# K of eleven head pairs loaded in chunk rows and transposed by DMA, Q in long rows re-laid by GpSimd, in a chunk-select attention with a gated MLP

## The chip, the cores and the metric

The kernel runs on one core of one Trainium2 chip. Its metric is the device time of one launch in microseconds (us); lower is better. Five engines work side by side, each through its own list of instructions in order: TensorE (PE) multiplies matrices and transposes into PSUM, VectorE (DVE) and ScalarE (ACT) read PSUM and SBUF, GpSimd (POOL) reads and writes SBUF, SyncE (SP) issues the DMA transfers, which 16 DMA engines carry out.

## The reference, cut to what matters

Attention over 32 pairs of batch and head (B = 4, H = 8, S = 768, D = 64), in which every query keeps the six best of the 24 chunks of 32 keys, and then an MLP with a hard-swish gate:

```python
k_chunks = k.reshape(B, H, nc, chunk, D)             # chunk = 32, nc = 24
k_min = np.min(k_chunks, axis=3)
k_max = np.max(k_chunks, axis=3)
ub = np.sum(np.maximum(q[:, :, :, None, :] * k_min[:, :, None, :, :],
                       q[:, :, :, None, :] * k_max[:, :, None, :, :]), axis=-1)
ub = np.where(causal, ub, -1000000000.0)
top_chunks = np.argsort(ub, axis=-1)[..., -top_k:]    # top_k = 6
scores = scale * np.matmul(q, k.transpose(0, 1, 3, 2))
scores = np.where(sel & (pos[:, None] >= pos[None, :]), scores, -1000000000.0)
attn = softmax(scores)
x = (attn @ v), heads side by side                    # 3072 x 512
h = x @ w_in                                          # 512 -> 2048
out = (h * np.clip(h + 3.0, 0.0, 6.0) / 6.0) @ w_out  # 2048 -> 512
```

## The kernel before, in words

Two heads of one batch make a pair; there are 16 pairs, four to a batch. Heads stand side by side on the 128 partitions (64 dimensions each). The MLP works on groups of 384 rows, eight of them, two to a batch; a group can begin once the four pairs of its batch have that half of their rows.

All work stands in one list, `ORDER`, written out by hand. A token such as `S.3.5.b` names an operation, its pair or group, its part and the PSUM slot it uses. Every engine takes its own tokens in the order of the list; waits come from what a token reads and overwrites. Two things therefore set the order around the change: the list, and the buffers. PSUM has three large slots, a, b and c (`PSB`, two banks each), and two small ones, x and y (`PSS`, one bank each).

For a pair `i` the tokens are:

- `lk`, `lq`, `lv` (L199 to L206): SP loads K, Q and V, two DMAs each, one for a head, in pieces of 64 numbers (256 bytes), so that a partition holds six positions 128 apart. Each of the three has three buffers (`KS`, `QS`, `VS`).
- `K`, `Q` (L263, L267): six transposes of 128 x 128 on TensorE into a large slot. `kb`, `qb` (L272, L275): ScalarE copies them as bf16 into `KB`, `QB` (three buffers each). `mx`, `mn` (L278): VectorE takes the maximum and the minimum of K over each chunk of 32 columns of that slot, into `KM`. `rp`, `rn` (L283, L286): the positive and the negative part of Q from column 192 on (the first six chunks need no choice).
- `U` (L296): the bounds, 24 small fp32 matmuls. `ub`, `T`, `t8`, `sel`, `L`, `mt`: causal bias, transposition, the eight largest, the comparison with the sixth, transposition back, and the mask rows `MT`.
- `S.i.u` (L368): the scores in six units, and `ex` (L382): their exponentials on ScalarE into `PT`.
- The mask goes in by one of two ways. Pairs without `sm` tokens (0 to 5) add it in PSUM by further matmuls with `EM` (L376), and GpSimd cuts the diagonal of the exponentials (`af`, L389). Pairs with `sm` (6 to 15, `PRODUCT`) write the mask rows to a scratch in HBM, four DMAs (L341), read them back widened over the partitions, six DMAs (`ml`, L346), into `MX` (parts of it lie in the weight buffers `WS`); GpSimd cuts the diagonal of that mask (`am`, L353), and VectorE multiplies the exponentials with it (`mu`, L360).
- `vc` (L251): GpSimd casts V. `A`, `B` (L405): values; `na`, `nb` (L422, L425): the division by the sums, into `XB`.

For a group `g`: `X` and `xe`, or three DMA transposes (`xt`, L431), turn `XB` into `XT`; `H` (L449, eight matmuls of 384 columns, 8 tokens to a group), `hu` (ScalarE, L457), `gt` (VectorE, L460), `O` (L466, four matmuls of 512 columns; four tokens make one 128-row output tile), `ot` (ScalarE, L474), `st` (L478, the store). Weights come through `wl` (SP) and `wc` (GpSimd).

Of the kernel before, what the change touches and what calls it, by code (L numbers as in the profile page):

```python
# [15 lines left out]
P = 128  # L16
# [18 lines left out]
PRD PRP lk.0 Z.b.14 PRA PRL K.0.a kb.0 mx.0 mn.0 lq.0 Q.0.b rp.0 qb.0 rn.0 lk.1 K.1.c kb.1 mx.1 lq.1 Q.1.a rp.1  # L35
qb.1 mn.1 lq.2 U.0.b ub.0 T.0.x Q.2.c rp.2 qb.2 rn.1 U.1.b lk.2 K.2.a kb.2 t8.0 sel.0 ub.1 L.0.y mt.0 S.0.5.b
rn.2 mx.2 mn.2 T.1.x ex.0.5 S.0.1.c ex.0.1 lq.3 lk.3 lv.0 vc.0 af.0.1 S.0.0.b ex.0.0 S.0.3.c ex.0.3 S.0.2.a
ex.0.2 U.2.b S.0.4.c ex.0.4 lv.1 t8.1 sel.1 L.1.y ub.2 T.2.x mt.1 S.1.1.b ex.1.1 S.1.4.a Q.3.c ex.1.4 S.1.0.b
t8.2 sel.2 L.2.y rp.3 qb.3 K.3.a kb.3 rn.3 af.0.0 af.0.3 af.0.2 af.0.5 B.0.0.x B.0.1.x mt.2 lq.4 lv.2 lk.5 lk.4
wl.0 lq.5 wl.1 ex.1.0 S.1.2.c ex.1.2 S.2.2.b ex.2.2 A.0.y mx.3 mn.3 S.1.5.c ex.1.5 S.1.3.a U.3.b ex.1.3 na.0  # L40
nb.0 ub.3 S.2.3.c ex.2.3 S.2.1.a S.2.0.b ex.2.1 ex.2.0 T.3.y t8.3 vc.1 af.1.0 vc.2 sel.3 af.1.1 af.1.2 af.1.3
af.1.5 af.2.2 K.4.c kb.4 mx.4 S.2.5.a ex.2.5 af.2.5 B.1.0.x af.2.1 af.2.3 Q.4.b rp.4 qb.4 L.3.y B.1.1.x mt.3
S.3.3.a ex.3.3 mn.4 rn.4 A.1.y S.2.4.c ex.2.4 nb.1 S.3.1.b ex.3.1 na.1 U.4.a S.3.0.c ex.3.0 S.3.5.b ub.4 T.4.x
t8.4 sel.4 wc.0 af.2.0 ex.3.5 af.3.5 wc.1 Q.5.a rp.5 S.3.2.c ex.3.2 X.0.0.y xe.0.0 K.5.b L.4.x mt.4 qb.5 lq.6
lk.6 lv.3 kb.5 B.2.0.y S.4.3.c rn.5 af.3.1 af.3.2 af.3.0 wl.2 B.2.1.y S.4.1.a vc.3 X.1.0.x ex.4.3 ex.4.1 S.4.2.c
ex.4.2 lv.4 wl.3 S.4.4.a ex.4.4 mx.5 mn.5 U.5.b af.3.3 wc.2 S.3.4.c xe.1.0 nb.2 ub.5 A.3.x na.3 ex.3.4 S.4.0.b
ex.4.0 vc.4 af.4.1 T.5.y t8.5 sel.5 Q.6.a rp.6 S.4.5.c ex.4.5 K.6.b L.5.x mt.5 B.3.0.y qb.6 rn.6 kb.6 mx.6 mn.6
S.5.2.c ex.5.2 A.2.x na.2 S.5.1.a ex.5.1 B.3.1.y nb.3 S.6.3.c ex.6.3 S.5.3.a ex.5.3 af.4.0 wc.3 U.6.b ub.6
S.6.0.c ex.6.0 A.4.x na.4 S.5.5.a S.6.1.b ex.5.5 ex.6.1 af.4.5 af.5.3 af.5.2 af.4.3 X.1.1.y xe.1.1 T.6.x wl.4
af.5.1 af.6.1 wc.4 S.6.4.c ex.6.4 lv.5 S.5.0.a ex.5.0 af.5.0 af.5.5 vc.5 lk.8 lk.7 lq.7 S.5.4.b ex.5.4 t8.6  # L50
X.0.1.y xe.0.1 sel.6 af.4.2 H.1.7.c H.0.7.a hu.1.7 gt.1.7 H.1.2.b wl.6 lq.8 hu.0.7 gt.0.7 L.6.y mt.6 sm.6 wl.5
hu.1.2 gt.1.2 K.7.c kb.7 mx.7 mn.7 B.5.0.x H.0.2.a hu.0.2 gt.0.2 H.0.1.b hu.0.1 A.5.y na.5 Q.7.c rp.7 gt.0.1
qb.7 rn.7 H.1.0.a wc.6 B.4.0.y B.4.1.y hu.1.0 S.6.2.b gt.1.0 ml.6.5 ml.6.2 ml.6.4 lv.7 wc.5 wl.7 lv.6 vc.7
ex.6.2 S.7.0.c ex.7.0 B.5.1.x nb.5 U.7.a ub.7 ml.6.0 ml.6.3 ml.6.1 K.8.b kb.8 nb.4 S.7.1.c ex.7.1 mx.8 mn.8
H.1.4.a hu.1.4 gt.1.4 H.1.3.c hu.1.3 gt.1.3 T.7.x t8.7 H.1.6.b H.0.6.a hu.1.6 gt.1.6 hu.0.6 H.0.4.c H.0.0.b
sel.7 gt.0.6 L.7.y hu.0.4 gt.0.4 Q.8.a mt.7 am.6.5 wc.7 af.6.0 vc.6 am.6.4 hu.0.0 gt.0.0 H.0.5.c H.0.3.b rp.8
qb.8 rn.8 hu.0.5 gt.0.5 U.8.a hu.0.3 sm.7 lk.9 S.8.4.c ex.8.4 am.6.2 am.6.3 ub.8 gt.0.3 O.0.2.0.x T.8.y t8.8
sel.8 S.6.5.a ex.6.5 lq.9 S.8.3.c S.7.5.b ml.7.1 ml.7.2 am.7.2 ml.7.3 ml.7.5 af.7.0 am.7.3 ml.7.0 mu.6.5 mu.6.1
# [12 lines left out]
S.10.0.a ex.10.0 S.10.5.c ex.10.5 O.1.1.0.y ex.11.1 T.11.x O.1.1.1.y am.9.4 am.9.3 t8.11 sel.11 mu.9.1 S.9.4.a
ex.9.4 am.9.2 mu.9.4 mu.9.5 S.11.0.c ex.11.0 S.10.1.b ex.10.1 O.1.1.2.y O.1.1.3.y ot.1.1 L.11.x S.11.5.a af.10.1
vc.9 am.9.5 ex.11.5 S.11.3.c K.12.b kb.12 ex.11.3 af.11.1 O.1.0.0.y ml.10.2 lv.10 ml.10.5 ml.10.4 af.10.0
am.10.4 am.10.5 mu.9.3 Q.12.a O.1.0.1.y mu.9.0 mu.9.2 mt.11 rp.12 mx.12 mn.12 H.2.7.c A.9.x hu.2.7 gt.2.7 vc.10
am.10.2 qb.12 rn.12 O.1.0.2.y O.1.0.3.y ot.1.0 S.11.2.b S.10.3.c ex.10.3 na.9 ex.11.2 U.12.a ub.12 B.9.0.y
B.9.1.y ml.10.3 am.10.3 mu.10.5 nb.9 S.10.4.c ex.10.4 S.12.3.a S.12.2.b ex.12.2 ex.12.3 O.2.2.0.x O.2.2.1.x
st.1.2 lq.14 ml.10.0 lk.13 lq.13 sm.11 lk.14 lv.11 ml.11.1 st.1.1 ml.11.3 ml.11.2 ml.11.0 mu.10.2 mu.10.0
mu.10.4 S.11.4.c S.12.5.b T.12.y t8.12 vc.11 ex.11.4 K.13.a kb.13 ex.12.5 O.2.2.2.x O.2.2.3.x ot.2.2 sel.12
mu.10.1 S.12.0.c S.12.1.b ex.12.0 ex.12.1 A.10.y xt.3 mu.10.3 B.10.0.x B.10.1.x am.11.3 af.12.0 am.11.2 af.12.1
af.11.0 mx.13 Q.14.c rp.14 mn.13 ml.11.5 nb.10 na.10 Q.13.b K.14.a kb.14 ml.11.4 st.2.2 O.2.0.0.x O.2.0.1.x  # L80
L.12.y mx.14 mn.14 qb.14 rp.13 qb.13 rn.14 mt.12 O.2.0.2.x O.2.0.3.x rn.13 ot.2.0 mu.11.0 mu.11.5 mu.11.1 st.2.0
st.1.0 lq.15 S.13.0.a S.13.2.c O.2.1.0.y ex.13.0 O.2.1.1.y ex.13.2 S.13.3.b ex.13.3 S.12.4.a am.11.4 am.11.5
S.13.4.c ex.13.4 A.11.x O.2.1.2.y na.11 xt.4 ex.12.4 U.13.b ub.13 U.14.c O.2.1.3.y mu.11.2 ub.14 T.13.x t8.13
# [31 lines left out]
def kernel(  # L115
# [83 lines left out]
    def load_k(i):  # L199
        load(KS[i % 3], k, i)  # L200

    def load_q(i):
        load(QS[i % 3], q, i)

# [321 lines left out]
```

## Time and profile before

| What | Value |
|---|---|
| median of 3 runs | 287.31 us (286.42 to 288.61) |
| the profiled execution, its own time | 287.24 us |
| its span on the core | 285.2 us |
| granted TensorE clock | 0.998 |
| first matmul of the MLP (H.1.7) | 56.5 us |
| last DMA out of the mask scratch | about 215 us |

The profile is one execution; its times are microseconds from the span's start. A row of a group gives the line, the engine, the operation, output and input by the program's names, the count, then the busy time and the mean in nanoseconds, and behind the second bar the time that the engine idled just before and what ended it. "SPq" is the DMA queue of SyncE at its issuing work. A row of a stage gives the stretch, its length, and then how long PE, its weight loads (PEld), DVE, ACT and POOL were busy in it, the granted clock, the mean share of the 16 DMA engines, and GB/s. The chain of work that ended last is followed backwards from the last instruction, at each step to what released it.

### The profile page before, as it was taken

Reading aid. Unit: us, or ns where it says so; the run is one execution under the profiler, and the core shown is the slowest. Engines: PE = TensorE matmul, PEld = TensorE weight load, DVE = VectorE, ACT = ScalarE, POOL = GpSimd, SP = SyncE. Lnnn points to the kernel's source line nnn. Section 1 sums busy time; section 2 is a strip of 40 time slices with the busy share of each in tenths; the row PEclk is TensorE's granted clock in tenths of the full one; section 3 lists DMA queues with packets and bytes.
Section 4 is the critical chain, followed back from the end, with each engine's and each line's share of the span. In section 5 each row is a group of like instructions: output and inputs, shape, how many; then the busy total and the mean of one; then the engine's idle time right before and its main releaser. Section 6 shows DMA issues by size and latency. Waiting matters only on the chain.

```text
span 285.2 us, 7112 instructions
## 1 busy us (share of the span) xinstructions
PE 273.7 (96%) x2782; PEld 165.5 (58%) x2782; DVE 205.1 (72%) x535; ACT 179.3 (63%) x234; POOL 72.5 (25%) x133
## 2 busy tenths in 40 slices
PE   8699999999999999999999889999999999999994
PEld 4467777667656576665574456555546645554541
DVE  4997787978989888989696788689748933251430
ACT  2599999977678874768787465352586324422521
POOL 6026575742450502314303100062422000000000
PEclk9999999999999999999999999999999999999999
DMA  8999999998999999979989958999594023110102
GB/s 169 218 214 191 344 219 305 288 261 239 261 247 253 224 254 213 231 206 274 245 184 233 259 105 173 271 255 237 148 280 142 12 47 93 74 39 37 61 15 110
DMA packets 107169, 54.40 MB, mean 191 GB/s; under 512 B 87168, under 2 KB 96128, under 8 KB 107136
## 3 DMA queue, kind: packets, MB, share of 16 engines
q1 hardware_dynamic: 107136, 53.95, 79.3%
q8 instruction: 22, 0.36, 0.6%
q14 instruction: 11, 0.09, 0.2%
HBM read 42.34 MB, written 9.24 MB: 181 GB/s over the span
## 4 chain that ended last, share of the span: by engine, by line
PE 61%; SPq 12%; DMA 9%; ACT 8%; DVE 4%; issue 4%; POOL 1%; ACTq 0%; POOLq 0%
PE PSx L466 13%; PE PSy L466 9%; PE PBa L449 7%; PE PBb L449 6%; PE PBc L449 6%; ACT PT L382 5%; SPq L346 4%; DMA VS<-in_v_dram 4%; SPq L341 3%; PE PSy L405 3%; SPq L197 3%; PE PBc L368 2%; DMA WS<-SCR 2%; PE PBb L368 2%; PE PBa L256 2%
## 5 line engine op out<-in xcount | busy, mean ns | idle before, releaser
L449 PEld LDWEIGHTS <-WIN 128*128 128x128 bf16 x512 | 49.1, 98 | 34.3 <-issue 2.5
L466 PEld LDWEIGHTS <-GT 128*128 128x128 bf16 x384 | 35.5, 98 | 39.6 <-issue 4.2
L466 PE MATMUL PSx<-WOUT,GT 128*128 128x512 bf16 x208 | 50.3, 379 | 0.0
L466 PE MATMUL PSy<-WOUT,GT 128*128 128x512 bf16 x176 | 43.5, 379 | 0.2 <-ACT OT L474 0.2
L382 ACT ACTIVATE PT<-PBc 128x1024 bf16<-128x1024 f32 (+2 forms) x38 | 37.0, 973 | 7.7 <-PE PBc L368 7.0
L449 PE MATMUL PBa<-XT,WIN 128*128 128x384 bf16 x176 | 32.2, 326 | 0.8 <-DMA XT<-XB 0.8
L460 DVE SCALAR_TENSOR_TENSOR GT<-U,PBc 128x768 bf16<-128x768 bf16 x21 | 20.0, 951 | 16.1 <-ACT U L457 16.1
L360 DVE TENSOR_TENSOR PT<-PT,WS 128x768 bf16<-128x768 bf16 (+2 forms) x70 | 30.3, 473 | 1.7 <-POOL WS L353 1.6
L449 PE MATMUL PBb<-XT,WIN 128*128 128x384 bf16 x168 | 30.7, 326 | 0.6 <-ACT PT L382 0.6
L449 PE MATMUL PBc<-XT,WIN 128*128 128x384 bf16 x168 | 30.7, 326 | 0.2 <-DVE UBX L301 0.2
L457 ACT ACTIVATE U<-PBa 128x768 bf16<-128x768 f32 x22 | 17.8, 810 | 20.8 <-PE PBa L449 19.5
L460 DVE SCALAR_TENSOR_TENSOR GT<-U,PBb 128x768 bf16<-128x768 bf16 x21 | 19.9, 949 | 14.0 <-ACT U L457 13.8
L405 PEld LDWEIGHTS <-PT 128*128 128x128 bf16 x672 | 24.6, 97 | 7.1 <-issue 1.4
L382 ACT ACTIVATE PT<-PBa 128x1024 bf16<-128x1024 f32 (+2 forms) x29 | 26.9, 927 | 2.1 <-PE PBa L368 2.1
L389 POOL TENSOR_SCALAR_AFFINE_SELECT PT<-PT 128x256 bf16<-128x256 bf16 x56 | 23.4, 439 | 15.6 <-ACT PT L382 15.6
L382 ACT ACTIVATE PT<-PBb 128x1024 bf16<-128x1024 f32 (+2 forms) x29 | 24.7, 852 | 2.7 <-PE PSy L405 1.8
L460 DVE SCALAR_TENSOR_TENSOR GT<-U,PBa 128x768 bf16<-128x768 bf16 x22 | 20.9, 949 | 7.6 <-ACT U L457 7.4
L457 ACT ACTIVATE U<-PBb 128x768 bf16<-128x768 f32 x21 | 17.0, 810 | 13.7 <-PE PBb L449 13.0
L457 ACT ACTIVATE U<-PBc 128x768 bf16<-128x768 f32 x21 | 17.0, 811 | 13.1 <-PE PBc L449 10.5
L353 POOL TENSOR_SCALAR_AFFINE_SELECT WS<-WS 128x256 bf16<-128x256 bf16 x30 | 13.3, 456 | 47.0 <-DMA WS<-SCR 46.8
L251 POOL CAST VB<-VS 128x768 bf16<-128x768 f32 x16 | 13.8, 862 | 38.1 <-DMA VS<-in_v_dram 35.9
L368 PEld LDWEIGHTS <-KB 64*128 64x128 bf16 x320 | 14.3, 94 | 13.0 <-issue 8.0
(103 smaller groups left out, 395.4 us busy)
## 6 DMA issues: line engine op xcount, KB each, us to landing
KS<-in_k_dram SPq DMA_DIRECT2D x32, 192.0 KB, 4.5
QS<-in_q_dram SPq DMA_DIRECT2D x32, 192.0 KB, 4.4
VS<-in_v_dram SPq DMA_DIRECT2D x32, 192.0 KB, 5.1
out_dram<-OT SPq DMA_DIRECT2D x24, 256.0 KB, 3.3
WS<-in_moe_w_in_dram SPq DMA_DIRECT2D x4, 1024.0 KB, 7.9
WS<-in_moe_w_out_dram SPq DMA_DIRECT2D x4, 1024.0 KB, 7.0
SCR<-MT SPq DMA_DIRECT2D x40, 72.0 KB, 3.2
MX<-SCR SPq DMA_DIRECT2D x10, 288.0 KB, 5.5
```

What stands on the lines that cost most here:

```text
L251: nc.gpsimd.tensor_copy(VB[i % 4][:, :, :, 0:D], VS[i % 3][:])
L346: nc.sync.dma_start(MX[i % 2][j][:, FIRST[j]:], src.unsqueeze(1).to_broadcast([16, 8, 2 * NQ - FIRST[j]]))
L353: nc.gpsimd.affine_select(out=T, in_=T, pattern=[[0, 2], [1, P]], compare_op=A.is_ge, fill=0.0, base=0, channel_multiplier=-1)
L360: nc.vector.tensor_tensor(out=T, in0=T, in1=mask_view(i, j, lo, q0 + n), op=A.mult)
L368: nc.tensor.matmul(PSB[c][:, e, at:at + n], lhsT=K[rows, j * P:(j + 1) * P], rhs=Q[rows, q0:q0 + n], start=True, stop=q0 + n <= Q0 or i in ...
L382: nc.scalar.activation(PT[i % 3][u][:, :, 0:n], PSB[slot["S", i, u]][:, :, 0:n], ACT.Exp, scale=float(scale))
L389: nc.gpsimd.affine_select(out=T[:, :, lo:lo + P], in_=T[:, :, lo:lo + P], pattern=[[0, 2], [1, P]], compare_op=A.is_ge, fill=0.0, base=0, ...
L405: nc.tensor.matmul(O[:, e, t, :], lhsT=PT[i % 3][u][:, e, lo:lo + P], rhs=VB[i % 4][:, j, e, :], start=(j == 0), stop=(j == qb))
L449: nc.tensor.matmul(PSB[c][:, ff, 0:GRP], lhsT=WIN[:, kt, (2 * f + ff) * P:(2 * f + ff + 1) * P], rhs=XT[g % 3][:, kt, :], start=(kt == 0), ...
L457: nc.scalar.activation(slot["R", g, f][:], PSB[slot["H", g, f]][:, :, 0:GRP], ACT.Relu, bias=3.0)
L460: nc.vector.scalar_tensor_tensor(out=GT[g % 2][:, 2 * f:2 * f + 2, :], in0=slot["R", g, f][:], scalar=6.0, in1=PSB[slot["H", g, f]][:, :, ...
L466: nc.tensor.matmul(PSS[c][:], lhsT=GT[g % 2][:, f, t * P:(t + 1) * P], rhs=WOUT[:, f, :], start=(f == 0), stop=(f == FT - 1))
```

## The change: what it does

Five things change together.

1. K of pairs 5 to 15 is loaded by one DMA into `KA`, 96 partitions with eight consecutive positions of both heads each (pieces of 2,048 bytes). VectorE takes maximum and minimum over the eight positions there (in SBUF, `MM`), TensorE transposes the two results into a small slot (two transposes of 96 columns), and VectorE reduces those by four to a chunk (`km`). GpSimd casts the rows to bf16 (`kc`, into the one buffer `KNB`), SP stores them to a scratch in HBM (`ks`), and a DMA transpose of 768 rows brings them into `KB` (`kt`). ScalarE's copy `kb` and the six transposes are not made for these pairs.
2. Q of all pairs is loaded by one DMA in pieces of 1,536 bytes (six consecutive positions of a head to a partition, two buffers `QA`). GpSimd re-lays it with the heads side by side (`qi`) into one buffer `QS`. After the transposition the columns stand in another order, so ScalarE (`qb`, `rp`) and VectorE (`rn`) read PSUM with a step of 128 columns.
3. V is loaded by one DMA in place of two, and has two buffers in place of three.
4. The mask goes by multiplication from pair 8 on; pairs 6 and 7 add it by matmul.
5. `ORDER` is written anew.

```diff
 ORDER = """
-PRD PRP lk.0 Z.b.14 PRA PRL K.0.a kb.0 mx.0 mn.0 lq.0 Q.0.b rp.0 qb.0 rn.0 lk.1 K.1.c kb.1 mx.1 lq.1 Q.1.a rp.1
...
-X.0.1.y xe.0.1 sel.6 af.4.2 H.1.7.c H.0.7.a hu.1.7 gt.1.7 H.1.2.b wl.6 lq.8 hu.0.7 gt.0.7 L.6.y mt.6 sm.6 wl.5
...
+PRD Z.b.14 PRP PRA PRL lk.0 K.0.a kb.0 mx.0 mn.0 lq.0 qi.0 Q.0.b rp.0 qb.0 rn.0 lk.1 K.1.c kb.1 lq.1 qi.1 Q.1.a
...
+B.0.0.x vc.1 lv.3 B.0.1.x lv.2 kc.5 qb.3 rn.3 af.1.1 S.1.5.a nb.0 ex.1.5 mt.2 S.1.0.b ex.1.0 mn.5 mx.5 S.1.4.a
+ex.1.4 S.1.2.b ex.1.2 A.0.x lq.5 lk.7 lk.6 ks.5 na.0 kb.4 U.3.a S.2.3.b ub.3 ex.2.3 mx.4 af.1.0 af.1.5 af.1.2
...
+mn.8 xe.1.1 xe.0.1 K.8.x km.8 X.0.0.y xe.0.0 ex.6.4 ex.6.3 Q.7.c af.5.1 af.5.3 qi.8 lq.10 kc.9 wc.2 af.4.0 wl.4
+mx.9 lv.6 mn.9 B.5.0.x A.5.y B.5.1.x lk.10 kt.7 ks.9 Q.8.b rp.7 qb.7 rn.7 na.5 rp.8 qb.8 rn.8 H.1.7.a hu.1.7
...
-    KS = ring(3, [P, NBLK, 2, D], FP32, "KS")
-    QS = ring(3, [P, NBLK, 2, D], FP32, "QS")
-    VS = ring(3, [P, NBLK, 2, D], FP32, "VS")
+    KP = S // 8
+    KSM = const.tile([P, 3 * S], FP32, name="KSM")
+    KS = [KSM[:, S * n:S * (n + 1)].rearrange("p (j e d) -> p j e d", e=2, d=D) for n in range(3)]
+    KA = [KSM[0:KP, 1024 * n:1024 * (n + 1)].rearrange("p (e k d) -> p e k d", e=2, d=D) for n in range(2)]
+    KNB = const.tile([KP, 8, 2, D], BF16, name="KNB")
+    MM = const.tile([KP, 2, 2, D], FP32, name="MM")
+    ROWQ = {int(t.split(".")[1]) for t in ORDER if t.startswith("qi.")}
+    QA = ring(2, [P, 2, NBLK, D], FP32, "QA") if ROWQ else []
+    QS = ring(1 if ROWQ else 3, [P, NBLK, 2, D], FP32, "QS")
+    VS = ring(2, [P, 2, NBLK, D], FP32, "VS")
...
+    ROWK = sorted({int(t.split(".")[1]) for t in ORDER if t.startswith("kt.")})
+    SK = {i: dram.tile([S, P], BF16, name=f"SK{i}") for i in ROWK}
...
     def load_k(i):
-        load(KS[i % 3], k, i)
+        if i in ROWK:
+            b, hp = divmod(i, NPAIR)
+            nc.sync.dma_start(KA[i % 2].rearrange("p e k d -> p e (k d)"),
+                              k[b, 2 * hp:2 * hp + 2].rearrange("e (p k) d -> p e (k d)", k=8))
+        else:
+            load(KS[i % 3], k, i)
+
+    def k_cast(i):
+        nc.gpsimd.tensor_copy(KNB[:], KA[i % 2].rearrange("p e k d -> p k e d"))
+
+    def k_store(i):
+        nc.sync.dma_start(SK[i][:].rearrange("(p k) c -> p (k c)", k=8), KNB[:].rearrange("p k e d -> p (k e d)"))
+
+    def k_turn(i):
+        nc.sync.dma_start_transpose(KB[i % 3][:], SK[i][:])
 
     def load_q(i):
-        load(QS[i % 3], q, i)
+        if i in ROWQ:
+            b, hp = divmod(i, NPAIR)
+            nc.sync.dma_start(QA[i % 2][:].rearrange("p e j d -> p e (j d)"),
+                              q[b, 2 * hp:2 * hp + 2].rearrange("e (p j) d -> p e (j d)", j=NBLK))
+        else:
+            load(QS[i % 3], q, i)
+
+    def q_interleave(i):
+        nc.gpsimd.tensor_copy(QS[0][:], QA[i % 2][:].rearrange("p e j d -> p j e d"))
 
     def load_v(i):
-        load(VS[i % 3], v, i)
+        b, hp = divmod(i, NPAIR)
+        nc.sync.dma_start(VS[i % 2][:].rearrange("p e j d -> p (e j) d"),
+                          v[b, 2 * hp:2 * hp + 2].rearrange("e (j p) d -> p (e j) d", p=P))
...
     def k_transpose(i, c):
         slot["K", i] = c
+        if i in ROWK:
+            for m in range(2):
+                nc.tensor.transpose(PSS[c][:, KP * m:KP * (m + 1)], MM[:, m].rearrange("p e d -> p (e d)"),
+                                    IDENT32[0:KP, 0:KP])
+            return
         transposes(KS[i % 3], PSB[c])
...
+    def q_cols(i, lo, t):
+        if i not in ROWQ:
+            return cols(slot["Q", i], lo, S), t[:]
+        return (cols(slot["Q", i], 0, S).rearrange("p (j x) -> p x j", x=P)[:, lo // NBLK:],
+                t[:].rearrange("p (x j) -> p x j", j=NBLK))
+
     def q_bf16(i):
-        nc.scalar.copy(QB[i % 3][:], cols(slot["Q", i], 0, S))
+        src, dst = q_cols(i, 0, QB[i % 3])
+        nc.scalar.copy(dst, src)
+
+    def k_bounds(i):
+        for m in range(2):
+            nc.vector.tensor_reduce(out=KM[i % 3][:, m, 0:NCH],
+                                    in_=PSS[slot["K", i]][:, KP * m:KP * (m + 1)].rearrange("p (c w) -> p c w", w=4),
+                                    axis=AX.X, op=(A.max, A.min)[m])
 
     def k_reduce(i, m):
+        if i in ROWK:
+            nc.vector.tensor_reduce(out=MM[:, m], in_=KA[i % 2].rearrange("p e k d -> p e d k"), axis=AX.X,
+                                    op=(A.max, A.min)[m])
+            return
...
     def q_plus(i):
-        nc.scalar.activation(RP[i % 2][:], cols(slot["Q", i], Q0, S), ACT.Relu)
+        src, dst = q_cols(i, Q0, RP[i % 2])
+        nc.scalar.activation(dst, src, ACT.Relu)
```

`rn` is changed as `rp` is, and `vc` reads V's new layout. In the new list the tokens ahead of the first H hold the scores of pairs 0 to 6 (before: all but two units of them), and the chunk reduces of pairs 0 to 9 (before: 0 to 6) and Q of pairs 0 to 8 (before: 0 to 6).

## The prediction

> **What bounds the kernel now.** I read the page first, then stage by stage the busy times, then the chain and the DMA queue's timeline where TensorE lost time.
>
> ```profile
> PE 273.7 (96%) x2782; PEld 165.5 (58%) x2782; DVE 205.1 (72%) x535; ACT 179.3 (63%) x234; POOL 72.5 (25%) x133
> ...
> DMA  8999999998999999979989958999594023110102
> ...
> q1 hardware_dynamic: 107136, 53.95, 79.3%
> ```
>
> A busy TensorE (PE) is not one at its peak, so 96% settles nothing. I took instead the shortest time that each kind of work needs when it runs on from other work, as the chain shows it: 1.30 us for an H (64 of them), 0.865 for an O (96), 0.66 for a K or Q transposition (32), 0.80 for a U (16), 0.41 for a T, 1.34 for A and B of a pair, 0.13 for an L, 0.34 for an X (4), 3.0 for the warm-up, and for the S of a pair 2,688 columns at H's pace (384 in 0.162 us), 1.12, with 1.01 more where the mask is added by matmul (2,432 columns, pairs 0 to 5). Sum: 83.2 + 83.0 + 21.1 + 12.8 + 6.6 + 21.4 + 2.1 + 1.4 + 3.0 + 17.9 + 6.1 = 258.6 us of the 285.2. I call the other 26.6 TensorE's loss. Set against the start times of the H in the order's own sequence, 14.2 us of it lie before the first H (56.5 us), 8.2 between there and 216 us, and some 4 at the very end.
>
> ```profile
> 7.40:56.50 49.10, 45.46 (x792) 33.34 (x793) 42.31 (x145) 44.93 (x59) 23.89 (x43) 1.00 1.11 254
> 56.50:113.50 57.00, 56.91 (x620) 36.41 (x618) 49.89 (x129) 41.85 (x54) 17.85 (x28) 1.00 1.01 245
> 113.50:162.40 48.90, 47.98 (x497) 28.27 (x496) 39.83 (x100) 36.08 (x47) 12.99 (x25) 1.00 1.00 235
> 162.40:216.00 53.60, 52.00 (x429) 29.06 (x429) 41.10 (x104) 29.44 (x39) 12.58 (x24) 1.00 0.90 213
> 216.00:282.00 66.00, 65.23 (x428) 35.41 (x424) 29.06 (x44) 24.68 (x35) 0.81 (x2) 1.00 0.18 54
> ```
>
> Stage by stage (after the length: PE, weight loads, VectorE (DVE), ScalarE (ACT), GpSimd (POOL), clock, DMA share): up to 56.5 us ScalarE is the bound, 44.9 of 49.1, with VectorE close behind at 42.3. From there PE is fed, VectorE stands at 81 to 88%, and the DMA engines have no room until 162 us. From 216 us PE alone counts. Where PE lost time in the middle, the chain goes through the DMA queue:
>
> ```profile
> 121.24 1.99 SPq L346
> ...
> 126.79 4.71 DMA out_dram<-OT
> ...
> 149.51 5.08 DMA WS<-SCR
> ...
> 163.13 1.25 SPq L431
> 164.43 1.40 SPq L431
> 165.87 0.62 SPq L341
> ```
>
> These are mask copies, an output store behind them, and transposes of XT issued late because SP was still at work on its list.
>
> **The change, part by part.** Pairs 5 to 15, K (11 pairs):
>
> ```profile
> L256 PE MATMUL PBa<-IDENT,KS 128*128 128x128 f32 x36 | 5.0, 275 | 0.0
> L272 ACT CAST KB<-PBa 128x768 bf16<-128x768 f32 x6 | 4.8, 802 | 5.5 <-PE PBa L256 4.8 <-DVE XB L425 0.6
> L278 DVE TENSOR_REDUCE KM<-PBa 128x24 f32<-128x768 f32 x12 | 10.9, 949 | 1.4 <-ACT KB L272 1.4
> L286 DVE TENSOR_SCALAR RN<-PBa 128x576 f32<-128x576 f32 x6 | 4.5, 756 | 0.9 <-ACT QB L275 0.9
> L251 POOL CAST VB<-VS 128x768 bf16<-128x768 f32 x16 | 13.8, 862 | 38.1 <-DMA VS<-in_v_dram 35.9 <-PE PBa L449 2.2
> ```
>
> - PE: six transposes of 128 columns go (0.66), two of 96 columns come. Four such in T take 0.33 in the chain, so two take 0.17; 0.25 with the start. 11 x 0.41 = 4.5 us less.
> - ScalarE: 11 casts of 0.80 go, 8.9 us.
> - VectorE: 22 reduces of 0.949 go, 20.9. In their place 22 reduces of 1,024 elements from SBUF with a step of 256 bytes, which no row shows. The line through L286 (576: 0.753) and L278 (768: 0.949) has 1.02 ns an element and 0.165 to start: 1.21 at 1,024. Ends: 0.95, the row itself, and 2.25, twice the time per element, as L360 shows when something holds its port (282 ns alone, 571 with GpSimd at work, 256 elements). I take 1.21, the nearest rows: 26.6. The 22 small reduces of 96 elements are 0.26 each by the same line, 5.8 (ends 0.19, the smallest PSUM row L422, and 0.36, twice the time per element).
> - GpSimd: a cast of 1,024 elements: 1.15 by L251's pace (0.94 by that of the weight casts, 1.89 for 2,048): 12.6. Q's 16 re-layings have the 768 elements of L251: 13.8 (ends 12 and 17, as both sides are fp32). Cover: GpSimd is busy 25% of the span, and at its fullest 11.8 of 15 us (45 to 60 us); if that cover goes, the causal cuts behind them on its queue come late, and A and B with them.
> - DMA queue: two K issues of a pair (1.6 at the median) become one load, one store and one transpose of 768 columns: 0.55 + 0.55 + 1.9 (1.26 for XT's 512, times 1.5; at least 1.3). Q: 1.5 becomes 0.55; V: two of 0.55 become one of 0.5 to 1.1. Pairs 6 and 7 lose four mask stores (2.5) and six loads (0.6 each). In all +15.4 -15.2 -2 -12.2 = 14 us less on SP; by the means, which hold the queue's own back-pressure, 24 less.
> - DMA engines: 226 us of 16 engines (79.3%). Packets of 256 bytes took 21.8 ns in the mean, of 1,408 to 1,664 bytes 85 to 95, of 2,048 95. K, Q and V were 73,728 of 256 bytes, 100 us; now 32,256 of them (44), 2,112 K rows (12.5), 4,096 Q rows (23), 1,056 of the store (6.3), 8,448 of the transposes (11.5): 97. The masks of two pairs take 13 away. With the semaphore packets some 17 less, still close to full until the masks end.
>
> Masks of pairs 6 and 7: by matmul 2 x 1.01 more on PE, the products (4.68 a pair: 4 x 0.59, 4 x 0.39, 2 x 0.39) off VectorE, 9.4; on GpSimd eight cuts of 0.46 change for eight of 0.44.
>
> ScalarE's and VectorE's reads of Q from PSUM now step by 512 bytes; no row shows such a read. I take the old times (0.655, 0.80, 0.753), as the element counts stay; the other end is twice the slope, 0.59 + 0.79 on ScalarE and 0.59 on VectorE a pair. A gain below nothing has no source: the same elements are read.
>
> Totals: PE -2.5, ScalarE -8.9, VectorE +2.1, GpSimd +26, SP -14 to -24.
>
> **By stage.** The new order has pairs 0 to 6 scored and the bounds of pairs 5 to 9 taken ahead of the first H. That puts 11.8 us more on VectorE before it (ten new reduces 12.1, eight small 2.1, two clippings of Q 1.5, less four old reduces 3.8) and 3.1 on ScalarE. VectorE's spans overlap by a tenth (its busy 205 against 222 by its means), so 42.3 + 10.7 = 53 from 7.4 us on: 60.4 with no gap, 63 at 95%. ScalarE needs 7.4 + 48/0.94 = 58.5. So **VectorE becomes the first stage's bound**, H begins to flow at about 62 instead of 56.5, and PE has 3.4 us more behind it by then: +2.1 net. In the middle VectorE then has 9.7 us less to do, SP 14 to 24 less: I give back 5 of the 8.2 us of loss there, the two places shown above. PE's own work: -2.5. Sum +2.1 - 5 - 2.5 = -5.4 on the profiled execution's 287.24 (its span 285.2 and 2.0 around it; the median shown is 287.31): **281.8, say 282**, 1.8% faster.
>
> K's longer way: load 4.5, cast 1.15, store 3.2 (as the mask stores land), transpose 1.9 and 3.8, some 14.6 us to the scores where it was 6. I cost it at nothing, since K rows are loaded two to three pairs ahead (7.8 us of ScalarE a pair); uncovered, every pair would wait some 3 us.
>
> [...] L278 reads neighbouring elements, and takes 1.02 ns each. [...]
>
> **Rivals.**
> 1. *Strided reduces at half pace (slower).* 2.25 each: ten ahead of the first H add 10.4 us where VectorE is the bound, and the twelve later 12.5 on a VectorE that has 9.7 less: 3 more. 282 + 13 = 295. It crosses 287 at about 1.7 us a reduce. For it: the step, and VectorE's 86%. Against: no row. If Q's reads double too, ScalarE gains 12 us ahead of the first H and the time passes 300.
> 2. *K comes late (slower).* SP works its list in order, so a transpose that waits for its store, or for the old scores of that KB buffer, holds loads of Q and V behind it; KNB, MM and QS are single. A hold of 1 us at each of the 11 pairs: 293.
> 3. *No gain.* PE's loss in the middle stays (VectorE at 88% and GpSimd's extra 26 us against L360's port), first stage +2.1, PE -2.5: 287.
>
> **How the numbers follow.** Forecast (277 to 284): 0.42. No gain (285 to 290): 0.18. Half pace (290 to 303): 0.28. K late: 0.12. Within 1% is about what a measurement of this kernel can tell from no change. So faster 0.42, same 0.18, slower 0.40. The forecast's own range is 277 to 284; both signs hold much, so the range given reaches from 277 to 300.
>
> **What would show it.** The new reduces' mean (1.2 or 2); first H at 60 to 63 us; VectorE over 90% and ScalarE under 90% up to it; Q's evictions at 0.65 and 0.80; SP idle between rows after 60 us; the scores of pairs 5 on not waiting for a DMA into KB; PE's busy row without the gaps at 126 and 160 us. I am wrong if reduces or evictions are slower by their step, or if SP stands on a transpose.

## The result, and the profile after

The changed kernel takes 301.12 us (median of 4, 299.48 to 301.55) where the kernel before took 287.14 beside it: a ratio of 1.047, 95% interval 1.041 to 1.053. It is slower, where 282 us was forecast. The profiled execution is the one of 299.48 us, with a span of 297.8.

First the page of the changed kernel: busy time by engine, the granted clock and the DMA engines in 40 slices, and the DMA queue's share.

```profile
PE 273.4 (92%) x2772; PEld 165.2 (55%) x2794; DVE 218.1 (73%) x537; ACT 171.3 (58%) x223; POOL 95.0 (32%) x160
...
PEclk9999899999999999997999999999999999999999
DMA  7999799699959999999997959766586031210022
...
q1 hardware_dynamic: 78336, 54.67, 76.8%
```

TensorE is as busy as before (273.4 to 273.7 us) in a span that is 12.6 us longer. ScalarE lost 8 us, GpSimd gained 22.5, both about as forecast; VectorE gained 13, not 2. The DMA queue moves 28,800 packets fewer, yet its packets take 76.8% of 297.8 = 228.7 us of 16 engines, where they took 226: the forecast 17 us less did not come.

The same stages as before (columns: length, then PE, weight loads, VectorE, ScalarE, GpSimd, clock, DMA share, GB/s):

```profile
7.40:56.50 49.10, 40.75 (x687) 30.04 (x686) 44.89 (x132) 39.22 (x51) 26.08 (x41) 0.97 0.99 247
56.50:113.50 57.00, 52.43 (x709) 35.66 (x710) 54.87 (x138) 41.31 (x53) 31.10 (x46) 1.00 1.02 241
113.50:162.40 48.90, 45.00 (x389) 26.14 (x392) 40.81 (x103) 26.42 (x35) 18.95 (x30) 0.97 1.13 231
162.40:216.00 53.60, 51.55 (x456) 29.17 (x461) 39.22 (x94) 28.93 (x38) 8.00 (x17) 1.00 0.77 182
```

VectorE has 44.9 of 49.1 us in the first stage and 54.9 of 57 in the second, so it looks like the bound of both; the first experiment bears that out for the first stage alone. TensorE has gaps in every one of the four. Counted as in the prediction (start of an H less the shortest time of the TensorE work ahead of it), its loss is 22.9 us at the first H, which starts at 68.6 us (14.3 at 56.5 before), and 37.5 at the first H of group 5 (22.4 before). So 8.6 us of new loss lie ahead of the first H and 6.5 in the middle, where 5 were to be given back. Together 15.1, less the 2.5 that TensorE's own work fell: the 12.6 us of the span.

The groups that the change adds or touches:

```profile
L331 DVE TENSOR_REDUCE MM<-KSM 96x128 f32<-96x1024 f32 x22 | 42.3, 1935 | 0.7 <-issue 0.7
...
L235 POOL COPY QS<-QA 128x768 f32<-128x768 f32 x16 | 13.2, 825 | 33.9 <-DMA QA<-in_q_dram 23.9 <-PE PBc L354 3.7 <-PE PBa L290 1.7
...
L218 POOL CAST KNB<-KSM 96x1024 bf16<-96x1024 f32 x11 | 12.9, 1170 | 24.9 <-DMA SK<-KNB 16.0 <-issue 5.3 <-DMA KSM<-in_k_dram 3.6
...
L321 ACT CAST QB<-PBc 128x768 bf16<-128x768 f32 x8 | 6.5, 806 | 0.0
...
L344 DVE TENSOR_SCALAR RN<-PBc 128x576 f32<-128x576 f32 x8 | 6.0, 750 | 2.3 <-ACT QB L321 2.3
...
L340 ACT ACTIVATE RP<-PBc 128x576 f32<-128x576 f32 x8 | 5.3, 658 | 4.9 <-PE PBc L290 4.9
...
L325 DVE TENSOR_REDUCE KM<-PSx 128x24 f32<-128x96 f32 x12 | 2.5, 247 | 0.0
```

All prices in these rows but one are those of the prediction: 0.825 and 1.17 us for GpSimd's copies (0.862 and 1.15), 0.81, 0.75 and 0.66 for the reads of Q from PSUM with a step of 512 bytes (0.80, 0.753, 0.655: that step costs nothing there), 0.247 for the small reduces (0.26). The one is the first row, 1.935 us for a reduce that was put at 1.21. GpSimd's idle time also shows a new wait: 16 us of its casts of K stood until the store of the pair before had left `KNB`.

Parts of the chain of waits, in order of time (start, duration, what):

```profile
96.85 1.86 DVE MM L331
...
106.79 4.62 DMA SCR<-MT
...
112.07 6.79 DMA QA<-in_q_dram
...
138.50 5.67 DMA WS<-SCR
...
145.97 5.17 SPq L212
...
153.77 4.53 DMA XT<-XB
```

Up to 104 us the chain goes again and again through the reduces of L331; after it through single transfers, and one issue of a load of K that alone held SP's queue for 5.17 us. The waits of SP ahead of K's transposition (L224) are there too:

```profile
SPq L224 <- ACT PT L440: 8.7, 3, 3.3
...
SPq L224 <- PE PBa L507: 5.0, 1, 5.0
...
SPq L224 <- DMA SK<-KNB: 2.6, 2, 1.8
```

### The profile page after: what moved, and what is told of

The parts are those of the page before. It is cut to its first block, busy times and chain, and to the rows that moved or that the text cites. A ratio compares the mean times of both kernels' runs of the same rounds, so it can differ in the third digit from the quotient of the medians.

```text
span 297.8 us, 7058 instructions
## 1 busy us (share of the span) xinstructions
PE 273.4 (92%) x2772; PEld 165.2 (55%) x2794; DVE 218.1 (73%) x537; ACT 171.3 (58%) x223; POOL 95.0 (32%) x160
## 3 DMA queue, kind: packets, MB, share of 16 engines
q1 hardware_dynamic: 78336, 54.67, 76.8%
## 4 chain that ended last, share of the span: by engine, by line
PE 59%; DVE 19%; DMA 11%; SPq 5%; issue 3%; ACT 2%; ACTq 0%; DVEq 0%
PE PSx L524 12%; PE PSy L524 9%; DVE MM L331 8%; PE PBc L507 8%; PE PBb L507 7%; PE PBa L507 6%; DMA WS<-SCR 4%; DMA QA<-in_q_dram 2%; DVE GT L518 2%; PE PBb L282 2%; SPq L212 2%; PE PSx L463 2%; PE PSy L463 2%; DMA SCR<-MT 2%; PE PBa L426 2%
## 5 line engine op out<-in xcount | busy, mean ns | idle before, releaser
L524 PE MATMUL PSy<-WOUT,GT 128*128 128x512 bf16 x211 | 52.3, 379 | 1.0 <-issue 0.5
L331 DVE TENSOR_REDUCE MM<-KSM 96x128 f32<-96x1024 f32 x22 | 42.3, 1935 | 0.7 <-issue 0.7
L440 ACT ACTIVATE PT<-PBa 128x1024 bf16<-128x1024 f32 (+2 forms) x34 | 30.7, 904 | 12.8 <-PE PBa L426 8.4
L524 PE MATMUL PSx<-WOUT,GT 128*128 128x512 bf16 x151 | 37.5, 379 | 0.5
L518 DVE SCALAR_TENSOR_TENSOR GT<-U,PBc 128x768 bf16<-128x768 bf16 x21 | 19.9, 949 | 21.8 <-ACT U L515 21.7
L507 PE MATMUL PBb<-XT,WIN 128*128 128x384 bf16 x176 | 33.1, 332 | 0.8 <-ACT OT L532 0.6
L440 ACT ACTIVATE PT<-PBb 128x1024 bf16<-128x1024 f32 (+2 forms) x33 | 30.1, 912 | 5.4 <-PE PBb L426 3.5
L515 ACT ACTIVATE U<-PBb 128x768 bf16<-128x768 f32 x22 | 17.8, 811 | 26.4 <-PE PBb L507 26.3
L507 PE MATMUL PBa<-XT,WIN 128*128 128x384 bf16 x168 | 30.7, 326 | 2.1 <-ACT PT L440 1.6
L440 ACT ACTIVATE PT<-PBc 128x1024 bf16<-128x1024 f32 (+2 forms) x29 | 27.6, 953 | 5.6 <-PE PBc L426 5.1
L418 DVE TENSOR_TENSOR PT<-PT,WS 128x768 bf16<-128x768 bf16 (+2 forms) x56 | 22.4, 438 | 7.7 <-POOL PT L447 4.0
L515 ACT ACTIVATE U<-PBa 128x768 bf16<-128x768 f32 x21 | 17.1, 813 | 14.3 <-PE PBa L507 14.3
L235 POOL COPY QS<-QA 128x768 f32<-128x768 f32 x16 | 13.2, 825 | 33.9 <-DMA QA<-in_q_dram 23.9
L426 PEld LDWEIGHTS <-KB 64*128 64x128 bf16 x320 | 15.1, 95 | 14.7 <-issue 9.2
```

The source lines that it names most:

```text
L235: nc.gpsimd.tensor_copy(QS[0][:], QA[i % 2][:].rearrange("p e j d -> p j e d"))
L331: nc.vector.tensor_reduce(out=MM[:, m], in_=KA[i % 2].rearrange("p e k d -> p e d k"), axis=AX.X, op=(A.max, A.min)[m])
L418: nc.vector.tensor_tensor(out=T, in0=T, in1=mask_view(i, j, lo, q0 + n), op=A.mult)
L426: nc.tensor.matmul(PSB[c][:, e, at:at + n], lhsT=K[rows, j * P:(j + 1) * P], rhs=Q[rows, q0:q0 + n], start=True, stop=q0 + n <= Q0 or i in ...
L440: nc.scalar.activation(PT[i % 3][u][:, :, 0:n], PSB[slot["S", i, u]][:, :, 0:n], ACT.Exp, scale=float(scale))
L507: nc.tensor.matmul(PSB[c][:, ff, 0:GRP], lhsT=WIN[:, kt, (2 * f + ff) * P:(2 * f + ff + 1) * P], rhs=XT[g % 3][:, kt, :], start=(kt == 0), ...
```

## The experiments

Three theories stood at the start: (A) the pace of the reduces is the whole loss; (B) it explains the first stage, and K's way through DRAM, SP's list and GpSimd's queue the rest; (C) the pace comes of the short runs of eight numbers, not of the step. Each ratio below is against runs of the kernel before on the same chip, with its 95% interval.

### The step of the reduces

```diff
-  nc.vector.tensor_reduce(out=MM[:, m], in_=KA[i % 2].rearrange("p e k d -> p e d k"), ...)
+  nc.vector.tensor_reduce(out=MM[:, m] (flat), in_=KA[i % 2] (flat).rearrange("p (g w) -> p g w", w=8), ...)
```

> The changed kernel with one thing altered: the 22 reduces of K rows read eight neighbouring numbers for each result in place of eight that lie 256 bytes apart. Count of elements, results and instructions are the same; the bounds, and so the chosen chunks, are not those of the reference. Theory A (the step of 256 bytes sets the reduces' pace, and that pace is the whole loss): the reduces fall from 1.94 to about 1.2 us, the first H from 68.6 us to 61 to 62, and the time to 284 to 288. Theory B (the pace explains the first stage only; the middle is lost to DMA round trips and SP): reduces 1.2, first H 61 to 62, time 291 to 295. Theory C (it is the short runs of eight per result, not the step): reduces stay at 1.9 and the time at 301.

295.26 us, ratio 1.033 (1.027 to 1.038). The reduces take 1.206 us, the 1.21 of the prediction; the first H starts at 63.0, with 17.3 us of loss. Behind it the loss up to group 5 stays: 15.1 us (32.4 less 17.3), where the change has 14.6. So VectorE was not the bound of the second stage, busy as it was. In the next run the reduces go altogether (`MM` is zeroed once):

> The changed kernel without the 22 reduces of K rows (their results are set to zero once, so the chosen chunks of pairs 5 to 15 are not the reference's; all else is as it was). VectorE is 42 us lighter. Theory A: VectorE is then nowhere the bound, first H at 57 to 59 us by ScalarE, time 276 to 282. Theory B: first H at 57 to 59 us, but the middle still loses some 12 to 15 us of TensorE to DMA and SP, time 287 to 291.

295.59 us, 1.034 (1.030 to 1.037): no better than with quick reduces. A falls: the step is worth 1.4% (4 us), nearly all of it ahead of the first H (68.6 to 63.0 us), and once it is gone the reduces cost nothing. Without them VectorE has 38.8 and ScalarE 43.7 of the 49.1 us of the first stage; ScalarE had 44.9 before. Then the four two-operand operations in place of a reduce:

```diff
+  KTR = max(src[:, :, 0:2], src[:, :, 2:4]); KTR = max(KTR, src[:, :, 4:6]); KTR = max(KTR, src[:, :, 6:8])
+  MM[:, m] = max(KTR[:, :, 0], KTR[:, :, 1])
```

> The changed kernel with each reduce of K rows replaced by four operations of two operands on neighbouring numbers (three of 256 elements, one of 128), the same maxima and minima. By the row of two-operand fp32 (384 elements 0.55 us, 1.02 ns an element) 3 x 0.42 + 0.29 = 1.55 us in place of 1.94, 8.5 us less on VectorE; GpSimd at work may slow them. Theory A: first H 3 to 4 us earlier, time 293 to 296. Theory B: time 296 to 299. If GpSimd's contention takes it back (both operands in SBUF): 300 to 303.

313.17 us, 1.094 (1.086 to 1.102): they took 0.762, 0.553, 0.659 and 0.569 us, 2.54 for a reduce of 1.94. The trace points to GpSimd. The 34 of these 88 operations that ran with no GpSimd operation beside them took what was expected, 0.41 to 0.42 us (256 elements) and 0.29 (128); the other 54 took 0.79 in the mean. The reduces of the change do not show this: 1.90 to 1.92 us for the four with GpSimd at rest, 1.91 to 1.99 for the 18 with it at work.

For the price by itself, single operations stand behind the end of the kernel, with nothing beside them:

> The changed kernel with rows to be measured put behind all its work, each twice, on dead buffers: fp32 reduces of 1,024 elements in SBUF with neighbouring groups of 8 and of 32, and with steps of 8, 16, 32, 256 bytes (groups of 8) and 128 bytes (groups of 32); a two-operand maximum of 512 elements; copies of 1,024 elements with a step of 512 bytes and without on VectorE, ScalarE and GpSimd. The time itself says nothing. If the step is what costs: neighbouring 1.2 us at both group sizes, 1.9 from the step on at which it begins. If the group size costs: 8 at 1.9 with every step, 32 at 1.2 with both.

| 1,024 fp32 elements in SBUF | us |
|---|---|
| VectorE reduce, eight neighbours | 1.21, 1.22 |
| the same, step 8 bytes | 1.22, 1.22 |
| the same, step 16 bytes | 1.98, 1.97 |
| the same, step 256 bytes | 1.87, 1.87 |
| reduce of 32 neighbours | 1.21, 1.22 |
| reduce of 32, step 128 bytes | 1.86 |
| VectorE tensor_scalar, neighbours / step 512 bytes | 0.69 / 1.25 |
| ScalarE copy, neighbours / step 512 bytes | 1.04 / 1.91 |
| GpSimd copy, neighbours / step 512 bytes | 1.04 / 1.92 |

C falls as well: runs of eight and of 32 cost the same (1.21 and 1.22 us). The price jumps between a step of 8 bytes (1.22 us) and of 16 (1.98), and does not grow after that (1.87 at 256). With the step a read takes 1.5 to 1.6 times as long in the reduces (16 to 256 bytes) and 1.8 in the other rows (512 bytes). VectorE's tensor_scalar may have another reason: with neighbours it runs at 0.68 ns an element where the reduce takes 1.2, and with the step at 1.22, so what it loses may be a quicker pace that it has with neighbours alone; this is an estimate from the two rows and was not taken apart. From PSUM ScalarE and VectorE read with 512 bytes of step at the old pace in the changed kernel (0.81, 0.66 and 0.75 us above, 0.80, 0.655 and 0.753 before).

### K's way through DRAM

The run with quick reduces, less K's cast and store; every transposition reads the scratch of pair 5:

```diff
-  ... kc.6 ... ks.6 ... (and so on to 15, out of the list)
-  nc.sync.dma_start_transpose(KB[i % 3][:], SK[i][:])
+  nc.sync.dma_start_transpose(KB[i % 3][:], SK[5][:])
```

> The run with neighbouring reduces (295.3), with K's cast and store left out for pairs 6 to 15; each transpose reads pair 5's scratch, so it is issued and moves the same bytes but waits for no store, and GpSimd's queue holds no cast that waits for the store before it. It leaves out the right K of ten pairs. Theory 1 (K's round trip through DRAM holds the rest: the cast waits for the store of the pair before, the cuts and casts behind it on GpSimd wait too, SP stands at the transpose): 287 to 290, first H at 58 to 60 us. Theory 2 (the rest lies in Q's and V's part, the masks and the order): 293 to 296.

290.61 us, 1.016 (1.008 to 1.024): another 1.6% is the cast and the store, with the waits for them; which of these was not taken apart. Next the transpositions go too:

```diff
-  kt.6 ... kt.15 (out of the list)
```

> The run without K's cast and store (290.6) with the transpositions of pairs 6 to 15 left out as well: nothing writes K's bf16 form for them, so K of ten pairs is not the right one. Theory 1 (each K transposition holds all 16 DMA engines about 1 us, as its 176 long packets in the trace suggest, and holds SP): 284 to 287. Theory 2 (the transposition is harmless once nothing waits for its store; what is left lies in Q's copy on GpSimd and the order): 289 to 292.

283.10 us, 0.986 (0.980 to 0.992). Ten transpositions are worth 3.0%, the largest single part. The third stage of the run with them, and of the one without (columns as above):

```profile
113.50:162.40 48.90, 41.98 (x366) 24.50 (x368) 34.78 (x92) 22.90 (x30) 12.16 (x24) 0.97 1.06 218
```

```profile
113.50:162.40 48.90, 48.23 (x452) 28.82 (x455) 41.51 (x103) 28.10 (x39) 10.91 (x17) 1.00 0.80 198
```

With them TensorE idles 6.9 us and the DMA engines are full (1.06); without them TensorE is fed and they have room (0.80). Two causes were possible: SP standing at a transposition until its `KB` is free, or the transposition itself. The last run keeps what each transfer waits for, the bytes and the buffers, and moves K with plain DMAs; those of `XT` are plain too, so `XT` of six groups holds other numbers:

```diff
-  nc.sync.dma_start_transpose(KB[i % 3][:], SK[5][:])
+  nc.sync.dma_start(KB[i % 3][:] as (p, j, c), SK[5][:].rearrange("(j p) c -> p j c", p=P))
-  nc.sync.dma_start_transpose(XT[...], XB[...])
+  nc.sync.dma_start(XT[...], XB[...] as (p, k, c))
```

> The run without K's cast and store (290.6) with plain DMAs of the same bytes in place of all transpositions by DMA, K's and XT's: the same waits on SP, the same buffers, 256-byte pieces; K of pairs 5 to 15 and XT of six groups of rows are not the right ones. SP has 29 issues of 0.6 in place of 1.3 us. Theory 1 (what holds is SP's wait until K's buffer is free): still 287 to 291, and the waits show SP standing at K's DMA for 15 us or more. Theory 2 (what holds is the transposition itself, its issue and its long packets): 280 to 285, and no more packets over 200 ns than before (78). XT's part alone can be worth some 2 us of either.

283.89 us, 0.986 (0.981 to 0.991), as quick as without these transfers, and TensorE is fed in the third stage:

```profile
113.50:162.40 48.90, 48.53 (x450) 28.64 (x450) 41.68 (x103) 28.45 (x38) 10.63 (x17) 1.00 0.90 220
```

So it is the transposition. SP still waits at K's DMA, 10.0 us in all, and that costs nothing; with the transpositions it was 20.3 us, so the wait did not stay the same in length. Its three longest:

```profile
SPq L220 <- PE PSx L297: 4.9, 1, 4.9
...
SPq L220 <- PE PBb L431: 2.1, 1, 2.1
...
SPq L220 <- ACT PT L437: 1.4, 1, 1.4
```

From the packet records: of the 49,920 packets of 256 bytes, 260 took over 200 ns in the run with transpositions, the longest 4.3 us, 16.0 us of all 16 engines together; with plain DMAs of as many packets none did, and their mean fell from 26.5 to 21.6 ns. The issue of K's DMA fell from 1.33 to 0.54 us at the median. `XT`'s part in this is small: the run without K's transpositions kept `XT`'s, had 86 such packets (78 before the change), and was as quick. How much of the 3% is the long issue and how much the long packets was not separated. Nor was it tried to give the changed kernel a fourth `KB`, or to keep the transpositions with nobody waiting for them.

Are the transpositions slow by themselves? Behind the end of the kernel before, single ones on an empty queue:

> The kernel before, and behind its end single DMAs with nothing beside them: three loads of Q in 256-byte pieces, four transpositions of 768x128 from DRAM, four of the same with a load of Q right behind, four transpositions of XT's shape from SBUF. Theory 1 (the transposition from DRAM itself holds the engines): about 16 packets of over 200 ns in each of them, and the load behind lands about 1 us later than alone. Theory 2 (the long packets come only of a full queue): none, and the load behind one is as quick as alone.

```profile
QS<-in_q_dram SPq DMA_DIRECT2D x12, 192.0 KB, 2.9
KB<-SKX SPq DMA_TRANSPOSE x8, 3.0
XT<-XB SPq DMA_TRANSPOSE x4, 2.4
```

They land in 3.0 us, as a plain load does in 2.9. A load right behind one was read by VectorE 2.4 to 3.1 us after the end of its issue, the last load by itself 2.4 us after. Around the eight from DRAM 34 packets took over 200 ns, none over 0.4 us; around the four from SBUF none. Neither theory held whole: some packets are long by themselves, but those of 1 to 4 us came only while the kernel ran.

### Q, V and the masks, each by itself

Q's part alone, in the list of before (`qi` put between `lq` and `Q`):

```diff
+  QA = ring(2, [P, 2, NBLK, D], ...); QS = ring(1, ...); one load in pieces of 1,536 bytes
+  nc.gpsimd.tensor_copy(QS[0][:], QA[i % 2][:].rearrange("p e j d -> p j e d"))   # qi.i
```

> The kernel before with only the Q part of the change: long rows into two QA, re-laid by GpSimd into one QS, read from PSUM with steps; K, V, masks and the order of the rest as before. Theory 1 (the Q part is harmless): 284 to 288; SP has 15 us less to issue and the DMA engines some 15 us less to move. Theory 2 (one QS and a GpSimd copy between the load and the transposition hold Q back, and GpSimd's 13 us slow VectorE's work in SBUF): 289 to 294, and the waits show Q's transposition behind GpSimd.

299.72 us, 1.051 (1.039 to 1.062): alone as dear as the whole change, with 16 issues fewer on SP. GpSimd's queue and TensorE's in that run (start, duration, work, and in brackets the idle time before and what ended it):

```profile
91.88 0.41 POOL L364 TENSOR_SCALAR_AFFINE_SELECT WS<-WS 128x256 bf16<-128x256 bf16 x1 [9.03 <-DMA WS<-SCR]
...
92.95 0.82 POOL L207 COPY QS<-QA 128x768 f32<-128x768 f32 x1
```

```profile
93.83 1.54 PE L260 MATMUL PBb<-IDENT,QS 128*128 128x128 f32 x6 [3.35 <-POOL QS L207]
```

The copy stands in GpSimd's list behind the causal cut of a mask that had to come from DRAM; GpSimd waited 9 us for it, Q's transposition waited for the copy, and TensorE for 3.35 us stood still. Q's load was not late: it had landed at 89.85 us. Before, that transposition (90.17 us) needed only its load. With the copies of pairs 7 to 15 on ScalarE, at the same places of the list:

```diff
+  (nc.gpsimd.tensor_copy if i < 7 else nc.scalar.copy)(QS[0][:], ...)
```

> The run with Q's part alone (299.7), with the copy of pairs 7 to 15 on ScalarE in place of GpSimd, at the same places of the list. Theory 1 (the copy is late because GpSimd's queue stands at causal cuts that wait for masks from DRAM, and TensorE idles and comes back at a lower clock): 286 to 290, and no dip of the granted clock. Theory 2 (one QS between the copy and the transposition, and the load's own time, hold Q back whichever engine copies): 296 to 301.

294.43 us, 1.022 (1.016 to 1.028): 8 of the 14 us (2.9 of 5.1 points) go. So GpSimd's queue was the larger part of that loss. The rest was not taken apart, but the trace shows the same thing on another engine: ScalarE's list stood 4.14 us at the copy of pair 9, until its load had landed (91.39 us), and TensorE 4.13 us for an exponential behind it; the granted clock of that run was 0.994, where it was 0.983 with all copies on GpSimd. Neither theory's range was met. The same edit in the changed kernel:

> The changed kernel with the copy of Q of pairs 7 to 15 on ScalarE in place of GpSimd, at the same places of the list. Theory 1 (GpSimd's queue, which waits 16 us for K's stores and 24 us for Q's loads, holds the change's middle as it held the run with Q's part alone): 293 to 297, the loss after the first H down by 4 to 8 us. Theory 2 (the change's own order keeps Q's copy clear of that; the reduces' step and DMA latencies hold it): 299 to 303.

302.36 us, 1.051 (1.042 to 1.061): nothing. In the change's own order the copies' place on GpSimd is not what holds it. There, Q's part undone makes things worse:

```diff
-  qi.0 ... qi.15 (out of the list; Q is loaded, transposed and read as before)
```

> The changed kernel with Q's part undone: two DMAs a pair of 256-byte pieces into three QS, no copy on GpSimd, PSUM read without steps; K, V, masks, the order of the rest and the reduces with the 256-byte step as in the change (301.1). Theory 1 (Q's copy stands in GpSimd's queue behind casts and cuts that wait for DMAs, and holds the transposition back): 291 to 296. Theory 2 (the middle is held by SP's list and the DMA engines, to which this gives back 16 issues and 32,768 packets): 301 to 306.

306.48 us, 1.064 (1.056 to 1.073). And once more, on top of the run without K's cast and store:

> The run without K's round trip (290.6; neighbouring reduces, no cast and store of K, transposes of pair 5's scratch, so K of ten pairs is not the right one) with Q's part undone as well. Theory 1 (the three causes add up: step of the reduces, K's round trip, Q's copy): 283 to 288, no slower than before. Theory 2 (SP and the DMA engines bind, and Q's old loads cost more than the copy): 290 to 295.

298.23 us, 1.035 (1.028 to 1.041), against 1.016. Both times Q's part is a gain of 1.7 to 1.8%, some 5 us: 16 issues and 20,736 packets fewer. (The expectation said 32,768 packets; that was miscounted.)

V's part alone, and the masks' part alone:

```diff
-  for e in range(2): nc.sync.dma_start(dst[:, :, e, :], ...)
+  nc.sync.dma_start(VS[i % 3] as (p, (e j), d), v[b, 2 * hp:2 * hp + 2].rearrange("e (j p) d -> p (e j) d", p=P))
```

> The kernel before with only the V part of the change: one DMA a pair in place of two, the cast reading it with heads outermost; three buffers, not two. The same packets of 256 bytes; sixteen issues fewer on SP (0.55 us each, 9 us). Where the middle's loss is SP's list: 284 to 287. Where one DMA's issue takes as long as the two, or the DMA engines are the limit: 286.5 to 288.

286.22 us, 1.000 (0.996 to 1.005).

> The kernel before with only the mask part of the change: pairs 6 and 7 take their masks by matmul, their stores, loads, cuts and products go (their causal cuts of the score tiles come in place). K, Q and V stay as they were, in the order of before. Theory 1 (the mask part is a gain of its own, as the prediction's sum has it: PE +2.0, VectorE -9.4, SP -12 and the DMA engines -13 us beside): 285 to 288, as VectorE and DMA are not the bound where the products stood. Theory 2 (what is left of the loss, some 8 us with no reduces at all, comes from the masks by matmul, as TensorE is the bound from there): 290 to 294.

287.64 us, 1.006 (1.001 to 1.011). In this run four of the six score units of pair 6 and two of pair 7 add the mask rows of an earlier pair, since they stand ahead of their own `mt` in the list of before; its matmuls are as many. 9.4 us less on VectorE and 12 on SP bring nothing where they stood, so it looks as if neither bound that stretch.

Last, K's part undone in the changed kernel, its transposes, casts and reduces put at the first free PSUM slot after the change's small ones:

> The changed kernel with K's part undone for all pairs: two loads, TensorE transposes, casts on ScalarE, and reduces from PSUM, put where the change has its two small K transposes; Q, V, the masks and the order of the rest as in the change. Theory 1 (K's part is the whole loss, and the rest of the change gains): 281 to 287. Theory 2 (K's part is some 9 us of the 14, and Q's copy and the order hold the rest): 290 to 294.

330.84 us, 1.149 (1.138 to 1.160), at a granted clock of 0.946. This tells nothing of K's part: the large transposes stand in slots that the list had not kept for them, and TensorE's longest waits there, 28.1 us in 13 of them, are for the reduces that read these slots. It also has five `KB` in place of three.

### The sum

| kernel | ratio | first H, us | TensorE's loss there | and at group 5 |
|---|---|---|---|---|
| before | 1 | 56.5 | 14.3 | 22.4 |
| the change | 1.047 | 68.6 | 22.9 | 37.5 |
| reduces without the step | 1.033 | 63.0 | 17.3 | 32.4 |
| and no cast and store of K | 1.016 | 62.1 | 16.4 | 29.5 |
| and no transpositions | 0.986 | 61.8 | 16.2 | 20.8 |

The steps were taken away in this order only; in another order their shares could differ. Together they account for all of the loss and more: without them the kernel is 1.4% quicker than before. These runs leave work out (the last one has no K in bf16 for ten pairs), so that 1.4% is no gain that could be had.

## Why the prediction was wrong

**The steps that failed are the price of the reduces and the sentence that costed K's longer way at nothing.**

- *Reduces at 1.21 us.* Measured 1.935. The mechanism was rival 1, the price between its 2.25 and the row taken, and past the 1.7 at which that rival put the crossing. Its worth was overstated: 13 us forecast for 2.25 are 7 for 1.935 by the same sum (ten reduces ahead of the first H at 0.725 us each; the later twelve stay within the 9.7 us), and the run without the step gave back 1.4%, 4 us. The rows taken, L286 and L278, read neighbouring elements of PSUM; with a step, reduces from SBUF took 1.87 to 1.98 us where they took 1.21 without, and the reads of Q from PSUM were no slower (0.81, 0.66 and 0.75 us). The 2.25 came from L360, 282 ns alone and 571 with GpSimd at work; that a port held it no trace shows, and the new reduces took 1.90 to 1.92 us with GpSimd at rest and 1.91 to 1.99 with it at work.
- *K's way of 14.6 us, costed at nothing.* That is the larger miss: from 1.033 to 0.986, 4.7%, 13.4 us, or 1.3 us for each of the ten pairs. Rival 2 had the place and nearly the size (a hold of 1 us a pair, 293), but its mechanism can hold for the smaller part alone: the single `KNB` and the store that the transposition waits for, at most 1.6%. The wait for the old scores of `KB`, which it also named, is in the run with plain DMAs too, and costs nothing there. The other 3% is the transposition itself, which the prediction priced as an issue of 1.9 us and 768 ordinary packets. The issue was cheaper (1.30 at the median); the packets were not ordinary.
- *DMA engines, 17 us less.* They took 2.7 more. The counts were right; 49,920 packets of 256 bytes at 26.4 ns, not 21.8, are 14.3 us of the difference, 10,336 of 2,048 bytes at 101.5, not 94.8, another 4.3. Packets over 200 ns account for most of the first: 254 with 17.3 us, where before had 78 with 4.4.
- *The rivals as alternatives.* Half pace gave 295 and K late 293, each alone, and the range ended at 300. Both came together: 1.4% and 4.7% on top of 0.986 are the 1.047 that was measured.
- *What held.* The rest of the sum: with quick reduces and K's way free the kernel runs at 0.986, which is 283.2 on the profiled execution's 287.24, where 281.8 was worked out. That is close in part by luck, as this run also lacks ten casts on GpSimd and ten stores and ten transpositions on SP, which the sum had counted. The first H was put at about 62 us and came at 61.8 there, with 16.2 us of loss; in the middle 4.6 us of loss are left (20.8 less 16.2), where 3.2 were forecast. That VectorE would be the bound of the first stage at 1.21 us is not borne out: without any reduce the first H came at 62.1, only 0.9 us earlier than with quick ones. ScalarE, with 43.7 of 49.1 us, is nearer to it.
- *Single terms.* GpSimd's copies, the reads of Q from PSUM and the small reduces came as priced. Q's part was a gain in the change's order and a loss in the order of before; the masks' part and V's, which the sum counted on for VectorE and SP, were no gain by themselves.

## What to carry to other kernels

Price a read from SBUF by its step: fp32 reduces on VectorE took 1.87 to 1.98 us with steps of 16 to 256 bytes and 1.21 without, and a step of 512 bytes made an operation 1.8 times as long on VectorE (0.69 to 1.25 us), ScalarE (1.04 to 1.91) and GpSimd (1.04 to 1.92). In PSUM the same step cost ScalarE (0.81 us for 0.80) and VectorE (0.75 for 0.753) nothing here, so re-order while evicting PSUM. A DMA transposition on a full queue is not its bytes: ten of them held this kernel for 3% (290.61 us with them, 283.10 without), and plain DMAs of the same bytes, behind the same buffers, for nothing (283.89); put plain ones in their place to learn what they cost. A copy put between a load and its user takes on the waits of the engine that copies (GpSimd stood 9.03 us here, and TensorE 3.35 behind it): find what stands ahead of it in that list.

## What the runs showed that was not expected

TensorE's granted clock fell to half around a short stall. In the run with Q's part alone, around the 3.35 us in which TensorE waited (granted clock: the third value from the right):

```profile
90.00:94.00 4.00, 0.65 (x6) 0.41 (x5) 3.07 (x6) 0.97 (x2) 2.12 (x5) 0.86 1.04 278
94.00:98.00 4.00, 3.78 (x25) 2.69 (x27) 0.76 (x1) 2.27 (x3) 0.85 (x3) 0.50 1.10 249
98.00:102.00 4.00, 3.85 (x44) 2.02 (x49) 1.69 (x5) 1.34 (x2) 0.00 (x0) 0.78 1.09 264
102.00:106.00 4.00, 3.95 (x61) 2.23 (x51) 3.21 (x9) 3.91 (x6) 2.85 (x4) 1.00 0.81 255
```

Half the clock for 4 us and 0.78 of it for the next 4 are 2.9 us lost behind a stall of 3.35: the six transposes of Q took 1.54 us, not 0.85. TensorE shows as busy all the while (3.78 and 3.85 of 4 us), so the busy row hides it. This wait of 3.35 us cost about twice its length. A later one in that run, of 2.76 us, cost nothing more: TensorE began again at 115.05 us, and the clock stayed at 1.00. What sets the two apart was not shown.

The changed kernel has such dips as well (the 8 and the 7 in its row of the clock): 0.50 from 34.39 to 37.80 us and from 136.79 to 140.20, and 1.00 in the 3.4 us ahead of each and behind it. In those ahead TensorE was busy for 1.74 and for 1.35 us, and no single wait in them was over 1.6 us. If the clock of the run with Q's part alone also went to half in one step, the 0.86 of its first row puts the fall at 92.9 us by estimate, 2.4 us after TensorE's last work (90.48).

TensorE was busy through both dips of the changed kernel, so each took 1.7 us of its time: 3.4 of the 12.6 us that the span grew. The prediction did not reckon with them.
